# Softmax reciprocals moved from VectorE to GpSimd, as a power of minus one, in a fused attention and two-layer MoE kernel

## The chip, the cores and the metric

The kernel runs on one core of a Trainium2 chip. The core has five engines with queues of their own, each of which works in order: TensorE (PE, with its weight loads shown as PEld), VectorE (DVE), ScalarE (ACT), GpSimd (POOL) and SyncE (SP), which here issues most DMAs. The metric is the device time of one execution in microseconds; lower is better. Three runs of the kernel before gave 962.45, 959.7 and 960.58 us, a median of 960.58.

## The reference

Attention with a block mask, then two feed-forward layers. Cut to what matters:

```python
# q, k, v: 4 batches, 8 heads, 576 positions, 64 features
scores = q @ k^T / sqrt(64); masked where block_i < block_j (blocks of 64)
attn = exp(scores - max)
attn = attn / (sum(attn) + 1e-9)
x = attn @ v                                  # 2304 tokens x 512
g = softplus(x @ w_in);  x = g @ w_out        # 512 -> 2048 -> 512
xn = x / sqrt(mean(x^2) + 1e-6) * rms_g
out = (silu(xn @ w_gate) * (xn @ w_val)) @ w_out2   # 512 -> 1536 -> 512
```

The changed step is the division by the sum of the exponentials.

## The kernel before

The work is done in fp32 accuracy, by splitting operands into a high and a low part and adding three products. Attention is cut into 48 units (batch, group of 192 queries, pair of heads), each with 3 tiles of 128 rows (64 queries of two heads). The unit's scores are computed tile by tile (`s_tile`): matmuls into a PSUM bank, the negated row maximum on DVE (L831), exp on ACT with the row sum as a side output (L868), and then `s_norm`. The first 12 units are "whole": they run in plain fp32, their P tiles are transposed on TensorE (L919), and the row factor is applied at the end, by a small matmul that reads the factors `nm[:, 4:7]` of all three tiles in `pv_whole` (L951 to L957). `s_norm` runs once per whole unit, three columns wide, and once per tile in the other 36 units, one column wide: 12 + 108 = 120 times.

In the other units the factor scales P into fp16 parts right away (`s_split`): the high part on ACT (L892, 84 times) or DVE (L891, 24 times), and the low part on DVE (L895). A zero-fill of the odd half block goes to GpSimd (L889, L897). When the third tile is done, one DMA transposes the parts `pst` into `pt` (L905), and the products with V follow six tiles later (LAG_T = 6).

`s_norm` is two instructions: the sum plus 1e-9, times a constant, on GpSimd (L876), and the reciprocal on DVE (L877), in place in `nm`. Its readers take the cell `(nm, "r", i)`.

While attention for the next 384 tokens runs, the first feed-forward layer of the tokens before is on the same engines: `g1` and `g2` fill PE between the attention matmuls. Attention ends at about 340 us; then follow the rest of the first layer and the second.

Nothing is emitted in the order in which it is written. `Plan.op` records each operation with an engine, a cost in us, a key and the cells that it reads and writes. `Plan.emit` schedules the list on a model of the engines up to 12 times and emits the order with the shortest modelled end. In the model each GpSimd operation that is no DMA holds a port that it shares with the DVE operations marked `port=True`. Operations with alternatives (`op2`) get their engine there too. A changed cost or engine can therefore move any instruction of the program.

`tops` is a small constant tile; its columns 0 to 27 hold the gain vector and column maxima of weights.

Of the kernel before, what the change touches and what calls it, by code (L numbers as in the profile page):

```python
# [8 lines left out]
FP32 = mybir.dt.float32  # L9
# [6 lines left out]
ALU = mybir.AluOpType  # L16
# [68 lines left out]
class Plan:  # L85
# [12 lines left out]
    def op(self, eng, dur, key, fn, reads=(), writes=(), done=0.0, nbytes=0, after=(), alt=(), cols=0.0, port=False):  # L98
        i = len(self.ops)
        if port:  # L100
            self.shared.add(i)
        if eng == "PE":
            self.cols[i] = cols
        if self.pin:
            self.pins[i] = key - self.pin
        if alt:
            self.alts[i] = ((eng, dur, fn),) + tuple(alt)
        deps, starts = set(), set(after)
        for c in reads:
            deps.update(self.writers.get(c, ()))  # L110
        for c in writes:
            deps.update(self.readers.get(c, ()))
            deps.update(self.writers.get(c, ()))
        for c in list(reads) + list(writes):
            b = c[0] if isinstance(c, tuple) else c
            if isinstance(b, Buf):
                if b.first is None:
                    b.first = i
                    if isinstance(b.ring, Banks):
                        self.takes[i] = b  # L120
                    if b.older is not None:
                        self.reuse.append((i, b.older))
                    else:
                        deps.update(b.ring.before)
                    if b.prev is not None:
                        starts.add(b.prev.first)
                else:
                    starts.add(b.first)
                b.users.append(i)
        for c in writes:  # L130
            if self.readers.get(c):
                self.writers[c] = [i]
                self.readers[c] = []
            else:
                self.writers.setdefault(c, []).append(i)
        for c in reads:
            self.readers.setdefault(c, []).append(i)
        deps.discard(i)
        self.ops.append((eng, dur, key, fn, deps, starts - deps - {i}, done, nbytes))
        return i  # L140
# [191 lines left out]
def t_act(n, sbuf=True):  # L332
    return (0.092 if sbuf else 0.05) + n * 0.836e-3
# [38 lines left out]
def kernel(  # L372
# [12 lines left out]
    nc = tc.nc  # L385
# [22 lines left out]
    op = plan.op  # L408

    const = ctx.enter_context(tc.tile_pool(name="const", bufs=1))  # L410
# [26 lines left out]
        return get  # L437

    ones = const.tile([128, 128], FP32, name="ones")
    tops = const.tile([128, 28], FP32, name="tops")  # L440
    gvec = tops[:, 0:KD]
    x_dram = {j: dram.tile([128, KD, 2, BLK], FP32, name=f"xd{j}") for j in range(NB)}
    y_dram = {j: dram.tile([128, KD, BLK], FP32, name=f"yd{j}") for j in range(NB)}
# [33 lines left out]
    def load(key, dst, src, reads=(), writes=(), nbytes=0, after=(), dur=0.45):  # L477
        return op("SP", dur, key, lambda: nc.sync.dma_start(out=dst(), in_=src), reads, writes, done=1.0, nbytes=nbytes, after=after)  # L478
# [212 lines left out]
    def aop(*args, **kw):  # L691
        att_ops.append(op(*args, **kw))

    def whole(u):
        return u < 12
# [10 lines left out]
    def load_k0(p, key):  # L706
        for c0, c1, cell in ((0, 192, k_cell(p)), (192, S, k_rest)) if p == 0 else ((0, S, k_cell(p)),):
            part_ = lambda c0=c0, c1=c1: k0(p)[:, c0:c1]
            att_ops.append(load(key, part_, kT[0, p][:, c0:c1], writes=[cell], nbytes=512 * (c1 - c0)))
            aop("ACT", t_act(c1 - c0), key, lambda part_=part_: nc.scalar.mul(part_(), part_(), 0.125), [cell], [cell])  # L710
            key += 0.25
# [13 lines left out]
    def load_q(u, key):  # L725
        b, g, p = units[u]
        cell, t = q_slot(u)
        att_ops.append(load(key, t, qP[b, g, p], writes=[cell], nbytes=196608, dur=0.63))
# [59 lines left out]
    def small(kind, fn, key, reads, writes):  # L788
        e = {"DVE": ("DVE", 0.07, lambda: fn(nc.vector)), "POOL": ("POOL", 0.245, lambda: fn(nc.gpsimd))}
        aop2([e[k] for k in kind], key, reads, writes, False)  # L790
# [3 lines left out]
    def s_tile(u, ib, key, after):  # L794
# [51 lines left out]
        if not 0:  # L846
            for x in todo:
                if whole(u):
                    s_turn(u, x[0], x[1], x[4])
                    continue  # L850
                s_norm(u, x[0], x[0] + 1, x[4])
                s_split(u, x[0], x[1], x[4])
            if whole(u) and ib == NG - 1:
                s_norm(u, 0, NG, key)
        elif ib == NG - 1:
            s_norm(u, 0, NG, key)
            for x in done:
                s_split(u, x[0], x[1], x[4])
# [13 lines left out]
    def s_norm(u, i0, i1, key):  # L872
        nm, done = part[u]
        key += 0.3
        cells = [(nm, "s", i) for i in range(i0, i1)]
        small(("POOL",), lambda e: e.tensor_scalar(nm()[:, 4 + i0:4 + i1], nm()[:, 4 + i0:4 + i1], 1e-9, 1.0 if whole(u) else 2.0**-14, ALU.add, ALU.mult), key, cells, [(nm, "t", i0)])  # L876
        aop("DVE", 0.08, key, lambda: nc.vector.reciprocal(nm()[:, 4 + i0:4 + i1], nm()[:, 4 + i0:4 + i1]), [(nm, "t", i0)], [(nm, "r", i) for i in range(i0, i1)])  # L877

    def s_split(u, ib, n, key):
        b, g, p = units[u]  # L880
# [477 lines left out]
    def when(t):  # L1358
        return when_[t] if t < len(when_) else when_[-1] + (t - len(when_) + 1)

    load_k0(0, 0.0)
    load_q(0, 0.1)
    load_q(1, 0.2)
# [138 lines left out]
    for s in range(len(steps) + LAG):  # L1502
        key = t_2 + s * step2
        if s < len(steps):
            j, f, i0, i1 = steps[s]
# [17 lines left out]
        if s >= LAG:  # L1523
            j, f, i0, i1 = steps[s - LAG]
# [70 lines left out]
```

## Time and profile before

| | |
|---|---|
| median of 3 runs | 960.58 us (959.7 to 962.45) |
| the profiled execution's own time | 959.8 us |
| span of its trace | 958.0 us |
| PE busy | 945.1 us |
| DVE busy | 724.4 us |
| ACT busy | 599.2 us |
| POOL busy | 50.8 us |

The profile is of one execution. The span runs from its first to its last instruction, and 1.8 us of the execution's time lie around it. Busy time of PE is partly modelled, since matmuls are pipelined. A row of the profile names the line of the kernel, the engine, the operation and the tiles; L464 is the one line that issues every matmul.

### The profile page before, as it was taken

How to read it: one execution, taken by the hardware profiler on the slowest of the kernel's cores; microseconds unless marked ns; L12 is line 12 of the kernel's file. 1: busy time of each engine (PE TensorE's matmuls, PEld its weight loads, DVE VectorE, ACT ScalarE, POOL GpSimd, SP SyncE). 2: the span in 40 equal slices, each digit the busy share in tenths (PEclk: the TensorE clock that was granted, in tenths of full speed). 3: DMA queues.
4: the chain of work that ended last, by engine and by line, in shares of the span. 5: the costliest groups of instructions: out<-in, count | busy, mean ns of one | idle time of the engine just before them, and what ended most of it. 6: DMA issues, size and time to landing. Idle time of an engine off the chain costs nothing.

```text
span 958.0 us, 19816 instructions
## 1 busy us (share of the span) xinstructions
PE 945.1 (99%) x7652; PEld 841.4 (88%) x7652; DVE 724.4 (76%) x1667; ACT 599.2 (63%) x1348; POOL 50.8 (5%) x220
## 2 busy tenths in 40 slices
PE   7999999999999999999999999999999999999998
PEld 5799899999999999999999997788887788877885
DVE  6989999987999859989845577786877754455455
ACT  7998887776778858778723454656564643433332
POOL 1101211111121000000000000000000000000000
PEclk9999999999999999999999999999999999999999
DMA  8654768988878656977576022223321200235322
GB/s 291 204 173 149 188 176 186 247 213 233 205 190 205 173 182 220 340 273 241 192 273 220 1 92 90 80 91 100 114 78 34 78 34 2 78 109 195 127 67 89
DMA packets 127663, 149.28 MB, mean 156 GB/s; under 512 B 86096, under 2 KB 100176, under 8 KB 126032
## 3 DMA queue, kind: packets, MB, share of 16 engines
q1 hardware_dynamic: 126992, 141.72, 48.8%
q0 software_dynamic: 576, 6.29, 1.8%
q8 instruction: 60, 0.98, 0.4%
q14 instruction: 35, 0.29, 0.1%
HBM read 98.44 MB, written 29.10 MB: 133 GB/s over the span
## 4 chain that ended last, share of the span: by engine, by line
PE 73%; DVE 1%; DMA 0%; ACT 0%; issue 0%; DVEq 0%; SPq 0%
PE b L464 73%; DMA wraw<-in_w2gv_dram 0%; DVE t L1078 0%; DVE g L365 0%; DVE pst L895 0%; ACT P L868 0%; DVE nm L831 0%; DVE pst L891 0%; DVE khl L757 0%; DVE wraw L1318 0%; DVEq L1590 0%; SPq L478 0%; DVE nm L833 0%; DVE nm L877 0%; DVE tops L564 0%
## 5 line engine op out<-in xcount | busy, mean ns | idle before, releaser
L464 PE MATMUL b<-x,w 128*128 128x192 f16 (+1 forms) x4176 | 482.9, 272 | 1.0 <-ACT P L868 0.9
L464 PEld LDWEIGHTS <-w 128*128 128x128 f16 x3024 | 250.5, 98 | 7.5 <-issue 0.2
L464 PE MATMUL b<-g,w 128*128 128x384 f32 x1152 | 225.1, 337 | 0.0
L464 PEld LDWEIGHTS b<-x,w 128*128 128x128 f32 x1152 | 199.5, 188 | 4.5 <-ACT P L868 1.7
L464 PEld LDWEIGHTS b<-g,w 128*128 128x128 f32 x1152 | 200.0, 188 | 1.5
L464 PE MATMUL b<-w,g 128*128 128x512 f16 (+1 forms) x654 | 145.4, 377 | 0.0
L464 PEld LDWEIGHTS <-g 128*128 128x128 f16 x654 | 63.6, 98 | 68.1
L1237 DVE TENSOR_TENSOR m<-m 128x384 f32<-128x384 f32 x72 | 40.1, 557 | 89.7 <-ACT m L1249 88.8
L1249 ACT COPY m<-b 128x384 f32<-128x384 f32 x108 | 51.8, 479 | 79.7 <-PE b L464 78.9
L868 ACT ACTIVATE P<-b,nm 128x288 f32<-128x288 f32 (+8 forms) x160 | 79.8, 501 | 13.5 <-DVE nm L831 9.6
L831 DVE TENSOR_REDUCE nm<-b 128x1 f32<-128x288 f32 (+8 forms) x160 | 70.5, 450 | 15.0 <-PE b L464 14.6
L355 ACT CAST g<-t 128x384 fp32r<-128x384 f32 x96 | 49.0, 515 | 36.6 <-PE b L464 34.1
L365 DVE TENSOR_TENSOR g<-t,g 128x384 fp32r<-128x384 f32 x96 | 52.7, 553 | 22.3 <-ACT g L355 21.9
L464 PE MATMUL b<-khl,qbd 128*128 128x448 f32 (+7 forms) x360 | 68.3, 312 | 0.2 <-ACT P L868 0.2
L895 DVE SCALAR_TENSOR_TENSOR pst<-P,nm,pst 128x320 f16<-128x320 f32 (+8 forms) x108 | 58.4, 546 | 5.0 <-ACT pst L892 4.2
L464 PEld LDWEIGHTS b<-khl,qbd 128*128 128x128 f32 x360 | 56.5, 188 | 3.0 <-ACT P L868 1.4
L892 ACT ACTIVATE pst<-P,nm 128x384 f16<-128x384 f32 (+8 forms) x84 | 47.8, 579 | 8.3 <-DVE nm L877 5.1
L1258 ACT ACTIVATE t<-b,fac 128x384 f32<-128x384 f32 x36 | 20.9, 580 | 40.0 <-PE b L464 39.8
L1273 ACT CAST g<-t 128x384 f16<-128x384 f32 x36 | 18.4, 512 | 41.9 <-DVE t L1272 41.9
L876 POOL TENSOR_SCALAR nm<-nm 128x1 f32<-128x1 f32 (+1 forms) x120 | 31.7, 264 | 220.7 <-ACT P L868 167.9
L1072 ACT ACTIVATE t<-b 128x384 f32<-128x384 f32 x51 | 24.9, 488 | 28.6 <-PE b L464 28.5
L1235 DVE TENSOR_TENSOR m<-b,m 128x384 f32<-128x384 f32 x72 | 39.9, 554 | 0.0
(137 smaller groups left out, 1159.8 us busy)
## 6 DMA issues: line engine op xcount, KB each, us to landing
wraw<-in_w2gv_dram SPq DMA_DIRECT2D x41, 512.0 KB, 4.4
wraw<-in_w_dram SPq DMA_DIRECT2D x25, 512.0 KB, 4.3
wraw<-in_w2o_dram SPq DMA_DIRECT2D x16, 512.0 KB, 4.8
qf<-in_qP_dram SPq DMA_DIRECT2D x42, 192.0 KB, 2.8
y<-yd SPq DMA_DIRECT2D x10, 768.0 KB, 6.1
xd<-x SPq DMA_DIRECT2D x32, 192.0 KB, 3.4
x<-xd POOLq DMA_DIRECT2D x4, 1536.0 KB, 8.4
xnd<-x SPq DMA_DIRECT2D x4, 1344.0 KB, 8.6
```

The lines of the kernel that those rows point to most:

```text
L355: "ACT": ("ACT", t_act(n), lambda: nc.scalar.copy(dst(), src())),
L365: "DVE": ("DVE", t_dve(n), lambda: nc.vector.tensor_tensor(dst(), a(), b(), ALU.subtract)),
L464: nc.tensor.matmul(o, lhsT=l, rhs=r, start=start, stop=stop, **kw)
L831: aop("DVE", t_dve(cn), key, lambda sp=sp, col=col, cn=cn: nc.vector.tensor_reduce(nm()[:, col:col + 1], sp()[:, :cn], axis=AX.X, op=ALU.m ...
L868: aop("ACT", 0.24 + cn * 0.836e-3, key, lambda sp=sp, col=col, c0=c0, cn=cn: nc.scalar.activation(P()[:, c0:c0 + cn], sp()[:, :cn], ACTF.E ...
L876: small(("POOL",), lambda e: e.tensor_scalar(nm()[:, 4 + i0:4 + i1], nm()[:, 4 + i0:4 + i1], 1e-9, 1.0 if whole(u) else 2.0**-14, ALU.add, ...
L892: "ACT": ("ACT", t_act(n) + 0.09, lambda: nc.scalar.activation(hi(), pc(), ACTF.Copy, scale=r())),
L895: aop("DVE", t_dve(n, True), key, lambda: nc.vector.scalar_tensor_tensor(lo(), pc(), r(), hi(), ALU.mult, ALU.subtract), [P, (nm, "r", ib) ...
L1072: op("ACT", t_act(BLK, False) + (1.28 if not sp_op else 0.0), key - 5, lambda: nc.scalar.activation(e(), h()[:, :BLK], ACTF.Softplus), [h] ...
L1235: op("DVE", t_dve(BLK), k, lambda: nc.vector.tensor_tensor(dst(), a(), b(), alu), rd, wr, port=o_sb(rd))
L1237: op2([("DVE", t_dve(BLK), lambda: nc.vector.tensor_tensor(dst(), a(), b(), alu)), ("POOL", t_pool2(BLK), lambda: nc.gpsimd.tensor_tensor( ...
L1249: op("ACT", t_act(BLK, False), key + 1, lambda o=o, s=s: nc.scalar.copy(s(), ps(o)()), [o], [s])
```

## The change

The reciprocal on DVE is replaced by an elementwise power on GpSimd, with a column of -1.0 as exponent. The column lies in four new columns of `tops` and is filled once by a memset on GpSimd. The operation's cost for the planner goes from 0.08 on DVE to 0.3 on POOL; its cells stay, with "minus" as one more input.

```diff
-    tops = const.tile([128, 28], FP32, name="tops")
+    tops = const.tile([128, 32], FP32, name="tops")
...
         small(("POOL",), lambda e: e.tensor_scalar(nm()[:, 4 + i0:4 + i1], nm()[:, 4 + i0:4 + i1], 1e-9, 1.0 if whole(u) else 2.0**-14, ALU.add, ALU.mult), key, cells, [(nm, "t", i0)])
-        aop("DVE", 0.08, key, lambda: nc.vector.reciprocal(nm()[:, 4 + i0:4 + i1], nm()[:, 4 + i0:4 + i1]), [(nm, "t", i0)], [(nm, "r", i) for i in range(i0, i1)])
+        aop("POOL", 0.3, key, lambda: nc.gpsimd.tensor_tensor(nm()[:, 4 + i0:4 + i1], nm()[:, 4 + i0:4 + i1], tops[:, 28:28 + i1 - i0], ALU.pow), [(nm, "t", i0), "minus"], [(nm, "r", i) for i in range(i0, i1)])
...
+    op("POOL", 0.1, 0.0, lambda: nc.gpsimd.memset(tops[:, 28:32], -1.0), [], ["minus"])
     load_k0(0, 0.0)
```

## Rows read from the trace of the kernel before

**Rows 1.** The page's first part: engine, busy us, share of span, instructions.

```profile
PE 945.1 (99%) x7652; PEld 841.4 (88%) x7652; DVE 724.4 (76%) x1667; ACT 599.2 (63%) x1348; POOL 50.8 (5%) x220
```

**Rows 2.** Busy time by stretch: us, PE, PEld, DVE, ACT, POOL, clock, DMA.

```profile
0.00:20.00 20.00, 13.44 (x95) 9.67 (x95) 11.29 (x30) 14.96 (x44) 1.78 (x14) 1.00 0.91 319
...
250.00:300.00 50.00, 49.89 (x424) 47.87 (x423) 46.34 (x141) 40.83 (x116) 8.99 (x39) 1.00 0.86 214
...
60.00:340.00 280.00, 278.26 (x2233) 262.45 (x2232) 248.59 (x685) 225.11 (x595) 41.73 (x184) 1.00 0.77 198
```

**Rows 3.** The chain that ended last: start us, length us, what.

```profile
255.56 698.59 PE b L464 x5723
```

**Rows 4.** Waits from 20 to 340 us: waiter <- releaser: us, times, longest.

```profile
ACT P L868 <- DVE nm L831: 9.6, 16, 1.9
...
POOL pst L889 <- DMA pt<-pst: 19.7, 10, 5.3
...
ACT pst L892 <- DVE nm L877: 5.1, 11, 0.9
PEld b L464 <- ACT P L868: 4.2, 11, 1.2
...
DVE nm L877 <- POOL nm L876: 3.8, 10, 1.1
...
PE b L464 <- ACT P L868: 1.3, 3, 0.9
...
PEld L464 <- DMA pt<-pst: 1.1, 2, 0.7
...
PEld L464 <- DVE nm L877: 0.2, 1, 0.2
```

**Rows 5.** Groups by line: the reciprocal and the one-wide sum.

```profile
L877 DVE RECIPROCAL nm<-nm 128x1 f32<-128x1 f32 (+1 forms) x120 | 18.5, 156 | 4.9 <-POOL nm L876 4.4
...
L876 POOL TENSOR_SCALAR nm<-nm 128x1 f32<-128x1 f32 x108 | 27.2, 252 | 177.3 <-ACT P L868 146.2 <-DVE nm L870 28.6 <-DVE g L365 0.7
```

**Rows 6.** Timeline, sums and reciprocals: first pair, one between, last of 108.

```profile
85.64 0.63 POOL L876 TENSOR_SCALAR nm<-nm 128x1 f32<-128x1 f32 x1 [3.54 <-ACT P L868]
86.36 0.15 DVE L877 RECIPROCAL nm<-nm 128x1 f32<-128x1 f32 x1
...
155.10 0.19 POOL L876 TENSOR_SCALAR nm<-nm 128x1 f32<-128x1 f32 x1 [1.35 <-ACT P L868]
...
156.07 0.15 DVE L877 RECIPROCAL nm<-nm 128x1 f32<-128x1 f32 x1
156.14 0.44 DVE L831 TENSOR_REDUCE nm<-b 128x1 f32<-128x288 f32 x1
...
156.44 0.67 ACT L892 ACTIVATE pst<-P,nm 128x448 f16<-128x448 f32 x1
...
332.55 0.19 POOL L876 TENSOR_SCALAR nm<-nm 128x1 f32<-128x1 f32 x1 [2.43 <-DVE nm L870]
332.96 0.15 DVE L877 RECIPROCAL nm<-nm 128x1 f32<-128x1 f32 x1
```

**Rows 7.** Timeline, the sum beside a two-operand DVE instruction.

```profile
150.18 0.75 DVE L895 SCALAR_TENSOR_TENSOR pst<-P,nm,pst 128x512 f16<-128x512 f32 x1 [0.35 <-ACT pst L892]
...
159.41 0.75 DVE L895 SCALAR_TENSOR_TENSOR pst<-P,nm,pst 128x512 f16<-128x512 f32 x1
159.58 0.63 POOL L876 TENSOR_SCALAR nm<-nm 128x1 f32<-128x1 f32 x1 [3.17 <-DVE nm L870]
```

**Rows 8.** Timeline, the first unit.

```profile
8.26 0.19 POOL L876 TENSOR_SCALAR nm<-nm 128x3 f32<-128x3 f32 x1 [7.28 <-ACT P L868]
...
8.48 0.18 DVE L877 RECIPROCAL nm<-nm 128x3 f32<-128x3 f32 x1 [0.56 <-POOL nm L876]
...
11.66 0.52 PE L464 MATMUL b<-ones,nm 128*64 128x64 f32 x12
...
13.56 0.55 PE L919 MATMUL b<-ones,P 128*128 128x128 f32 x3 [1.38 <-ACT P L868]
```

## The prediction

> **What bounds the kernel now.** I read the busy times first. TensorE (PE) is busy in 945.1 us of the span, VectorE (DVE) in 724.4, ScalarE (ACT) in 599.2 and GpSimd (POOL) in 50.8 [rows 1]. Shares over the span mix stages, so next come the stretches [rows 2]. The changed lines run only while attention runs, up to 333 us. In the stretch from 60 to 340 us PE is busy for 278.26 of 280 us at a granted clock of 1.00, DVE for 248.59 and ACT for 225.11. From 250 to 300 us DVE is busy for 46.34 of 50. So PE sets the pace, and DVE is the next engine to run out of time. The reader is to see that PE's open idle time in that stretch is 280 - 278.26 = 1.74 us. The first 20 us hold 20 - 13.44 = 6.56 us more.
>
> The chain that ended last says the same from the other end [rows 3]. From 255.56 us on it is one piece of PE work, 698.59 us long. What a wait costs after 255.56 us did not decide the end in that execution. An edit in attention can only move the end by what it does to PE's waits before that, or by making a new one.
>
> Third, I asked who waited for whom from 20 to 340 us [rows 4]. PE's longest group of waits is for the exp on ACT, 1.3 us in 3 times. The weight loads (PEld) wait for the exp for 4.2 us and for the DMA transpose for 1.1 us. The exp itself waits for the row maximum on DVE (9.6 us in 16 times). So a freer DVE does have a way to PE: maximum earlier, exp earlier, PE's bank free earlier. The reciprocal stands as a releaser of weight loads with 0.2 us, once. ACT's scaling of P (L892) waits for it for 5.1 us in 11 times out of 84, and only 10 times in 120 did DVE sit idle for the sum of GpSimd, 3.8 us in all.
>
> **The change part by part.** *Reciprocals taken off DVE.* 120 of them go, 18.5 us of recorded busy time, 156 ns each [rows 5]. But DVE starts its next instruction before one has ended: in the example of [rows 6] the reciprocal starts at 156.07 and the maximum behind it at 156.14. So each one costs the DVE queue 0.07 us. That is 120 x 0.07 = 8.4 us, of which the 108 one-wide ones of the later units make 7.6 us. This lies on an engine that is not the bound. It is worth to PE at most what PE waits for the chain through DVE and exp.
>
> *Powers added to GpSimd.* 120 instructions with two operands in SBUF. The trace has no power and no two-operand instruction on GpSimd. From below: the sum's own small instruction on GpSimd has a mean of 252 ns one-wide [rows 5], and 0.19 us when nothing disturbs it [rows 6]; a power can hardly be cheaper. From above, the long cases of the one-wide sum take 0.63 us, at 85.64 and 159.58 [rows 6, 7], and a power with such a delay and twice the sum's own work on top would come to 0.63 + 2 x 0.19, about 1 us. The diff's own cost line says 0.3, a number for ordering and no measurement. I take 0.35 us, nearer the undisturbed row, since only one value in each partition is worked on, and keep 0.19 and 1.0 for the range. The load on GpSimd, 120 x 0.35 = 42 us, fits: from 60 to 340 us it is busy for 41.73 of 280 us [rows 2].
>
> *The latency from sum to factor.* Now the reciprocal stands in the queue of a busy DVE. I took the gap from the end of each sum to the start of its reciprocal for all 108 one-wide pairs; first and last are in [rows 6] (gaps 0.09 and 0.22), and so is one with 0.78. The mean is 0.45 us. With its own 0.155 the factor is there 0.61 us after the sum. Afterwards the power starts right behind the sum on the same engine, say 0.05 us later, the gap that an undisturbed hand-over in this trace shows ([rows 8], 8.45 to 8.48, gives 0.03). That makes 0.05 + 0.35 = 0.40 us: 0.2 us sooner. With 0.19 it is 0.24, with 1.0 it is 1.05, which is 0.44 us later. The break-even is a power of 0.56 us.
>
> *The port.* At 159.58 the sum takes 0.63 us, and ends as the two-operand DVE instruction beside it (L895 from 159.41, 0.75 us) ends. The L895 with the same shape at 150.18, which has no GpSimd work beside it, takes 0.75 us as well [rows 7]. So here GpSimd waits and DVE does not pay. The Trainium skill's "GPSIMD Engine Reference", section "Specifications", says that GpSimd shares its SBUF interfaces with VectorE and contends with instructions that have two SBUF inputs; this trace agrees on the 0.63 against 0.19, and the rule speaks against the change: it would put a second instruction of each tile into that contention. By the rows a power that meets one is delayed by up to 0.44 us, and by none where the sum has just waited it out, as it comes directly behind it. I count 0.06 us per power, the mean excess of the sum (252 - 192), inside the 0.35. For DVE I count nothing.
>
> *Order in the queues.* The planner is given another engine, 0.3 in place of 0.08, and a dependence between two GpSimd instructions. It lists the whole program anew, so any engine's order may shift, and with it the choice between DVE and ACT for the scaling. I can't cost that from rows. I allow 3 us either way, a little over what all PE idle time of the stretch amounts to. The memset of the -1 column falls into GpSimd's idle first 8 us [rows 8] and costs nothing; without that cover it would cost one instruction of 0.2 us.
>
> *First units.* The factor of the first unit is ready at 8.66 and first read by PE at 11.66 [rows 8]: 3.0 us of cover over the longest price taken above. No loss there.
>
> *Sum.* The freed DVE time and the shorter hand-over make the exp come a little sooner. I give PE back the 1.3 us that it waited for the exp [rows 4], and none of the weight loads' 4.2, because those loads overlap running matmuls. From the profiled execution's own 959.8 us this gives 958.5. The three runs have a median of 960.58, 0.8 above it; on that scale it is 960.6 - 1.3 = 959.3 us. A measurement of this kernel tells about 0.3%, 2.9 us, from no change; so this is no change.
>
> **The rivals.** *DVE is the hidden bound* (faster). For it: 46.34 of 50 us in the densest stretch, and exp waiting for DVE 9.6 us. If all of PE's 1.3 and the weight loads' 4.2 us behind the exp go, the time is 960.6 - 5.5 = 955.1. Against it: the stretch shows only 1.74 us of open PE idle time, and from 255.56 us nothing but PE decides.
>
> *The power is slow* (slower). Price 1.0 us, decisive from 0.56 up. The factor then comes 0.44 us later than now, and behind ACT's L892 stand, in order, the next exps and the copies that feed PE. 84 x 0.44 = 37 us of ACT waits at worst, against 280 - 225.11 = 54.9 us of ACT idle time [rows 2]. ACT would have little left; if one in seven of these microseconds reaches PE, an estimate, that is 5.3 us: 965.9. Against it: most scalings start later than the factor is ready, as only 11 of 84 waited for it.
>
> *Head of line on GpSimd* (slower). The zero-fills of pst wait in the same queue for the DMA transpose, 19.7 us in 10 times, longest 5.3 [rows 4]. If the new order puts such a fill between a sum and its power, the power waits with it. A few waits of 5.3 us, each covered in part by the lag of six tiles between scores and values, would give about 4 us: 964.6. Before, the reciprocal on DVE could not be caught so, only the sum.
>
> *First use pays once* (no change still). The first power may take longer than the rest, if its code has to be fetched. Unit 0 has 3.0 us of cover between 8.66 and 11.66; what goes beyond it delays PE, less what PE would have idled anyway (1.38 us at 13.56 [rows 8]). It leaves the band of 2.9 us only where the first power takes over 3.0 + 2.9 = 5.9 us with nothing absorbed; a first power between 3.0 and 5.9 us gives up to 963.5. Against it: the first sum on GpSimd took 0.19 us [rows 8], with no pause in front of it that the trace puts down to code. The Trainium skill's "GPSIMD Engine Reference", section "Instruction dispatch", gives the first call of a freshly loaded GpSimd kernel about 6 us that a profile shows no instruction for; by it the time would be an estimated 963.5 before anything is absorbed, and no run here shows it yet.
>
> **How the numbers follow.** Forecast (within 0.3%): 0.43, with the first-use rival's 0.05 in the same band: same 0.48. DVE as hidden bound, or an order that falls out well: faster 0.29. Slow power 0.13 and head of line or a worse order 0.10: slower 0.23. The range goes from just under the DVE case, 954.5, to the slow-power case, 965.9, rounded to 966. The likeliest case alone is 957.7 to 962.
>
> **What would show it.** Right: the powers last 0.25 to 0.45 us; ACT's wait for the factor (L892) falls under 5.1 us; DVE from 60 to 340 us has 7 to 16 us less recorded busy time (0.07 us each if overlaps are counted once, 0.155 if not); PE idle there stays between 0.5 and 3 us; the sum's own duration stays near 0.25. Wrong: powers of 0.6 us or more, and ACT's waits for GpSimd above 15 us in the list of waits; fills ahead of powers in the timeline; PE waiting for the transposes; or an attention stage that ends more than 3 us from 340 us in either direction.

## The result and the profile after

The changed kernel takes 967.66 us (median of 6 runs, 964.5 to 969.7) against 960.9 us: a ratio of 1.0063, interval 1.0048 to 1.0078. It is slower by about 6 us. The forecast was 959.3 us and no change; 967.66 lies above the range's 966.

The page's first part, of the kernel after:

```profile
PE 949.6 (98%) x7652; PEld 842.3 (87%) x7652; DVE 716.3 (74%) x1544; ACT 600.0 (62%) x1351; POOL 125.8 (13%) x341
```

DVE did lose its load: 716.3 us against 724.4 [rows 1], 8.1 us less, where 8.4 were forecast. GpSimd went from 50.8 to 125.8 us, 75 us more, where 42 were forecast. Busy time by stretch (us, PE, PEld, DVE, ACT, POOL, clock, DMA share, GB/s) answers to [rows 2]:

```profile
0.00:20.00 20.00, 13.73 (x87) 9.36 (x88) 10.28 (x23) 14.30 (x43) 4.67 (x18) 0.91 0.90 323
60.00:340.00 280.00, 277.07 (x2192) 259.82 (x2191) 242.03 (x572) 228.48 (x601) 108.60 (x295) 1.00 0.76 195
```

From 60 to 340 us PE is idle for 2.93 us against 1.74, and issues 41 matmul records fewer. GpSimd is busy for 108.60 of 280 us. Its groups by line are next; L877 is the power, one and three columns wide, L876 the sum. They answer to [rows 5]:

```profile
L877 POOL TENSOR_TENSOR nm<-nm,tops 128x1 f32<-128x1 f32 x108 | 64.6, 601 | 7.5
L876 POOL TENSOR_SCALAR nm<-nm 128x1 f32<-128x1 f32 x108 | 27.8, 257 | 121.7 <-ACT P L868 94.0 <-DVE nm L870 18.1 <-DVE am L770 4.3
L877 POOL TENSOR_TENSOR nm<-nm,tops 128x3 f32<-128x3 f32 x12 | 11.6, 964 | 0.7
```

A power has a mean of 601 ns where 350 were taken. Over the 108 pairs, the way from the end of the sum to the end of the power is 0.80 us on average; to the end of the reciprocal it was 0.60 us. The waits from 20 to 340 us (us in total, times, longest) answer to [rows 4]:

```profile
ACT pst L892 <- POOL nm L877: 16.3, 27, 1.4
...
POOL pst L889 <- DMA pt<-pst: 12.9, 8, 3.3
...
ACT P L868 <- DVE nm L831: 10.7, 17, 1.4
...
PEld b L464 <- ACT P L868: 5.8, 11, 1.4
...
DVE pst L891 <- POOL nm L877: 4.2, 10, 1.0
...
PE b L464 <- ACT P L868: 2.6, 4, 1.1
```

The reader is to see the wait of ACT's scaling for the factor, 5.1 us before and 16.3 now, and below it PE's own wait for the exp doubled, 1.3 to 2.6. Of these 2.6 us, though, 2.0 fall before 105 us, where it was 0.2 before the change and where few of the powers lie. The exp's wait for the maximum has not shrunk (9.6 to 10.7), although DVE is freer.

That is not the whole of it, though. L1017 copies a unit's result from PSUM, so its first and last start date the first split unit and the last. The source view of before and after (durations, then first and last start in us):

```profile
L1017 ACT ACTIVATE x<-b,dall x36: 397/416/457, 105.0 to 343.2; 128x192 fp32r<-128x192 f32 x36
```

```profile
L1017 ACT ACTIVATE x<-b,dall x36: 397/418/462, 108.6 to 349.7; 128x192 fp32r<-128x192 f32 x36
```

The changed kernel is 3.6 us late by the first of these copies, when 22 of the 120 powers have run, and 6.5 us late at the last. Something else besides the power is slow, and the new listing of the program is the suspect.

### The profile page after: what moved, and what is told of

Its sections match the earlier page's. It is cut to its first block, busy times and chain, and to the rows that moved or that the text cites. A ratio compares the mean times of both kernels' runs of the same rounds, so it can differ in the third digit from the quotient of the medians.

```text
span 966.0 us, 19810 instructions
## 1 busy us (share of the span) xinstructions
PE 949.6 (98%) x7652; PEld 842.3 (87%) x7652; DVE 716.3 (74%) x1544; ACT 600.0 (62%) x1351; POOL 125.8 (13%) x341
## 4 chain that ended last, share of the span: by engine, by line
PE 54%; DVE 5%; ACT 3%; DMA 2%; issue 1%; POOL 0%; DVEq 0%; ACTq 0%
PE b L464 54%; DVE w L607 1%; DMA m<-in_w2o_dram 1%; DVE wg L365 1%; DMA wraw<-in_w_dram 1%; DVE w L365 1%; DMA m<-in_w2gv_dram 1%; DVE g L365 1%; ACT wraw L505 1%; DVE wg L508 0%; ACT wa L506 0%; ACT w L355 0%; DVE wa L508 0%; ACT w L606 0%; ACT g L355 0%
## 5 line engine op out<-in xcount | busy, mean ns | idle before, releaser
L464 PE MATMUL b<-g,w 128*128 128x384 f32 x1152 | 228.2, 339 | 1.2 <-DVE y L1132 0.9
L868 ACT ACTIVATE P<-b,nm 128x288 f32<-128x288 f32 (+8 forms) x160 | 79.6, 501 | 13.2 <-DVE nm L831 10.7
L877 POOL TENSOR_TENSOR nm<-nm,tops 128x1 f32<-128x1 f32 (+1 forms) x120 | 76.2, 637 | 8.2
L895 DVE SCALAR_TENSOR_TENSOR pst<-P,nm,pst 128x64 f16<-128x64 f32 (+8 forms) x108 | 57.7, 547 | 12.0 <-ACT pst L892 11.5
L892 ACT ACTIVATE pst<-P,nm 128x128 f16<-128x128 f32 (+8 forms) x89 | 51.1, 580 | 17.3 <-POOL nm L877 16.3
L876 POOL TENSOR_SCALAR nm<-nm 128x1 f32<-128x1 f32 (+1 forms) x120 | 31.6, 263 | 155.2 <-ACT P L868 116.3
L505 ACT ACTIVATE wraw<-wraw 128x512 int32<-128x512 uint32 x50 | 33.9, 679 | 11.7 <-DMA wraw<-in_w_dram 7.1
```

What stands on the lines that cost most here:

```text
L464: nc.tensor.matmul(o, lhsT=l, rhs=r, start=start, stop=stop, **kw)
L505: op("ACT", t_act(CW), prio, lambda: nc.scalar.activation(lw().bitcast(I32), lw(), ACTF.Copy, scale=0.874 * 2.0**-29, bias=0.5), [raw], [( ...
L868: aop("ACT", 0.24 + cn * 0.836e-3, key, lambda sp=sp, col=col, c0=c0, cn=cn: nc.scalar.activation(P()[:, c0:c0 + cn], sp()[:, :cn], ACTF.E ...
L877: aop("POOL", 0.3, key, lambda: nc.gpsimd.tensor_tensor(nm()[:, 4 + i0:4 + i1], nm()[:, 4 + i0:4 + i1], tops[:, 28:28 + i1 - i0], ALU.pow) ...
L892: "ACT": ("ACT", t_act(n) + 0.09, lambda: nc.scalar.activation(hi(), pc(), ACTF.Copy, scale=r())),
L895: aop("DVE", t_dve(n, True), key, lambda: nc.vector.scalar_tensor_tensor(lo(), pc(), r(), hi(), ALU.mult, ALU.subtract), [P, (nm, "r", ib) ...
```

## The experiments

Two theories stood from here. *Price*: the power takes GpSimd too long, the factor is late, ACT and with it PE wait. *Order*: the planner, told another engine and cost, lists a program that is worse whoever computes the reciprocal. "Old order" below means that the planner was told the kernel before, so that PE, ACT, SP and the rest of DVE keep that kernel's order; only the instruction behind the reciprocal's entry is another. "New order" is the listing of the changed kernel. Ratios are to runs of the kernel before on the same chip, each with its 95% interval.

**Old order, with the power.**

```diff
-aop("DVE", 0.08, key, lambda: nc.vector.reciprocal(...), ...)
+aop("DVE", 0.08, key, lambda: nc.gpsimd.tensor_tensor(..., tops[:, 28:28 + i1 - i0], ALU.pow), ...)
...
+nc.gpsimd.memset(tops[:, 28:32], -1.0)     # ahead of everything
```

> The planner is told the old story (0.08 us on DVE), so TensorE, ScalarE, SyncE and the rest of DVE keep the order of the kernel before; only the reciprocal itself runs as a power on GpSimd. Theory price (the power lasts 0.54 to 0.64 us where 0.3 was planned, ACT and DVE wait for it, TensorE idles): 965 to 969 us, and the 16 us of waits of L892 for the power come back. Theory order (the newly listed order is worse whoever computes the reciprocal): 959 to 962 us.

Measured: 967.72 us, 1.007 (1.0055 to 1.0085). The price theory's number. The loss starts where the one-wide powers start, as the copies show:

```profile
L1017 ACT ACTIVATE x<-b,dall x36: 400/415/453, 105.7 to 351.7; 128x192 fp32r<-128x192 f32 x36
```

At the first copy it is 0.7 us late, at the last 8.5. How it comes about is best seen in one stretch, first in the kernel before (timeline: start us, length, engine, line):

```profile
109.22 0.15 DVE L877 RECIPROCAL nm<-nm 128x1 f32<-128x1 f32 x1
...
109.87 0.19 ACT L868 ACTIVATION_READ_ACCUMULATOR P<-b,nm 128x1 f32 x1
109.96 0.95 ACT L892 ACTIVATE pst<-P,nm 128x256 f16<-128x256 f32 x2
...
110.15 0.19 POOL L876 TENSOR_SCALAR nm<-nm 128x1 f32<-128x1 f32 x1 [0.63 <-ACT P L868]
...
111.41 0.16 DVE L877 RECIPROCAL nm<-nm 128x1 f32<-128x1 f32 x1
...
111.68 0.61 ACT L892 ACTIVATE pst<-P,nm 128x384 f16<-128x384 f32 x1
111.83 1.49 PE L464 MATMUL b<-x,w 128*128 128x384 f32 x7 [0.93 <-ACT P L868]
```

Then the same tiles in the old order with the power:

```profile
109.95 1.44 POOL L877 TENSOR_TENSOR nm<-nm,tops 128x1 f32<-128x1 f32 x2
...
110.59 0.19 ACT L868 ACTIVATION_READ_ACCUMULATOR P<-b,nm 128x1 f32 x1
...
110.91 1.07 ACT L892 ACTIVATE pst<-P,nm 128x256 f16<-128x256 f32 x2
111.34 0.31 POOL L897 MEMSET pst<- 128x256 f16 x1
...
111.73 0.26 POOL L876 TENSOR_SCALAR nm<-nm 128x1 f32<-128x1 f32 x1
...
112.04 0.20 POOL L889 MEMSET pst<- 128x128 f16 x1
...
112.21 0.76 POOL L877 TENSOR_TENSOR nm<-nm,tops 128x1 f32<-128x1 f32 x1
...
112.90 0.44 PE L464 MATMUL b<-x,w 128*128 128x384 f32 x1 [1.28 <-ACT P L868]
113.00 0.62 ACT L892 ACTIVATE pst<-P,nm 128x384 f16<-128x384 f32 x1 [0.16 <-POOL nm L877]
```

Before, the row sum is read out by 110.06, and GpSimd takes it up 0.09 us later. With the power, the row sum is there at 110.78, but GpSimd is in the second of two powers and then in a fill; the tile's sum starts at 111.73, 0.95 us later, another fill follows, and the power ends at 112.97. From row sum to factor it is 2.2 us, where it was 1.5. ACT's scaling of this tile waits for it and starts at 113.00. PE's wait for the exp there is 1.28 us in place of 0.93, but it ends at 112.90, before this power does. It goes back to the two powers ahead, from 109.95 to 111.39: ACT's scalings of their tiles start 0.32 us after the start of the row sum's read-out, where it was 0.09, and take 1.07 us in place of 0.95, and only then comes the next exp. So in this stretch the tiles come in a burst, and GpSimd's queue is the thing that is late.

**New order, reciprocal back on DVE; new order, a cheap instruction on GpSimd.**

```diff
 # in the changed kernel; the entry stays ("POOL", 0.3), only what it issues changes
-lambda: nc.gpsimd.tensor_tensor(..., ALU.pow)
+lambda: nc.vector.reciprocal(...)                                       # one kernel
+lambda: nc.gpsimd.tensor_scalar(..., constant, 1.0, ALU.mult, ALU.mult)  # the other
```

> The order of the changed kernel on every engine, but the reciprocal runs on DVE as before (0.155 us), at the place in the list that the power had. Theory price: 959 to 962 us, as the slow instruction is gone. Theory order: 966 to 969 us, with the split of the first tile (L895) still starting near 95 us and not near 89.

> The order of the changed kernel, the instruction stays on GpSimd, but is a multiplication by a constant (about 0.2 us) in place of the power: the reciprocal is left out of the computation, factors and results are others. Theory price: 959 to 962 us. Theory order: 966 to 969 us. Between the two only the duration on GpSimd differs from the changed kernel.

Measured: with the reciprocal on DVE 967.09 us, 1.0069 (1.0052 to 1.0085); with the cheap instruction 963.63 us, 1.0028 (1.0017 to 1.0039). Neither theory alone gives both: the first lies in the range of the order theory, the second between the two ranges. The cheap one leaves 2.7 us of loss with no power in the kernel: that is the new order. The first is worse than that by about 4 us, although nothing slow is left on GpSimd and the old order carries the same reciprocals. The new order was listed without them on DVE; that this is the reason is not shown, as ACT waits for the factor there for only 7.0 us, near the 5.1 of the kernel before.

Where the order loses can be seen by stretch (as in [rows 2]). From 20 to 105 us, the kernel before, the changed kernel, and the cheap instruction in the new order:

```profile
20.00:105.00 85.00, 84.26 (x675) 72.80 (x673) 78.97 (x201) 78.92 (x208) 10.71 (x42) 1.00 0.55 170
20.00:105.00 85.00, 81.26 (x634) 68.83 (x632) 76.62 (x175) 75.32 (x194) 20.80 (x53) 1.00 0.53 164
20.00:105.00 85.00, 81.47 (x632) 69.01 (x631) 77.21 (x177) 75.88 (x198) 13.17 (x56) 1.00 0.55 168
```

PE is idle for 0.74, 3.74 and 3.53 us there, while only 19 and 20 of their 120 powers or multiplications run by then. Over all kernels of this document, those below included, it is 0.6 to 1.0 us in the old order and 1.6 to 4.1 in the five other listings, whatever computes the factor. From 105 to 350 us it is the other way round. The kernel before, the changed kernel, the cheap instruction in the new order, and the power in the old order:

```profile
105.00:350.00 245.00, 243.29 (x1949) 230.98 (x1946) 210.22 (x585) 191.05 (x504) 36.01 (x161) 1.00 0.80 200
105.00:350.00 245.00, 243.65 (x1958) 230.39 (x1957) 203.68 (x480) 192.29 (x514) 97.98 (x266) 1.00 0.79 197
105.00:350.00 245.00, 244.72 (x1967) 232.10 (x1966) 202.95 (x482) 192.64 (x512) 59.68 (x264) 1.00 0.79 199
105.00:350.00 245.00, 239.49 (x1881) 224.24 (x1878) 202.64 (x476) 186.50 (x497) 95.86 (x261) 0.99 0.79 196
```

Here PE is idle for 1.71, 1.35, 0.28 and 5.51 us. In the old order the power's price shows as 3.8 us of idle time of PE, in the new order as 1.1 us (1.35 against 0.28).

**Changed kernel, the planner told the measured durations.**

```diff
-aop("POOL", 0.3, key, ...
+aop("POOL", 0.55 if i1 - i0 == 1 else 0.95, key, ...
```

> The changed kernel with the measured durations told to the planner (0.55 us one column wide, 0.95 three wide, in place of 0.3), so the order is listed anew around the real price. Theory price: part of the loss goes, 961 to 965 us. Theory order: a new order is a new draw, anywhere from 957 to 970 us, and no reason to lie near the kernel before.

Measured: 967.13 us, 1.0068 (1.0053 to 1.0083). A listing that knows the price does not avoid it. The expectation of the price theory, that a part of the loss would go, was wrong.

**Old order, a cheap instruction on GpSimd.** As the first experiment, with the multiplication by a constant in place of the power.

> The order of the kernel before, and on GpSimd behind the sum a multiplication by a constant (about 0.2 us) in place of the power; the reciprocal is left out of the computation. Beside the old order with the power (967.7 us) only the duration on GpSimd differs. Theory price: the loss goes, 958.5 to 962 us, L892 waits 3 to 6 us for it. Theory hand-over (it is the move to GpSimd that costs, whatever its duration: one more instruction in its queue, its port): 965 to 968 us.

Measured: 961.05 us, 1.000 (0.9987 to 1.0014). Moving the step to GpSimd is harmless when it is short, and the 8 us taken off DVE buy nothing either.

**Two new listings of the kernel before.**

```diff
-aop("DVE", 0.08, key, lambda: nc.vector.reciprocal(...
+aop("DVE", 0.07, key, lambda: nc.vector.reciprocal(...     # and 0.10 in a second kernel
```

> Nothing but the planner's cost of the reciprocal changes, from 0.08 to 0.07 us: the same instructions on the same engines, listed anew. Theory order (a new listing alone moves the time by some us): up to 5 us from 960.9 in either direction, most likely upwards. If a new listing is harmless: 959.5 to 962.5 us.

> As the one before with a cost of 0.10 us: a second redraw of the order with no other change. Theory order: up to 5 us from 960.9 in either direction, and not the same as the first. If a new listing is harmless: 959.5 to 962.5 us.

Measured: 964.6 us, 1.0042 (1.0025 to 1.0058), and 964.2 us, 1.0029 (1.0015 to 1.0042). The same instructions, but for the choice between ACT and DVE for the scaling of P (84 on ACT before, 80 and 79 in these two), and 3 to 4 us slower for a hundredth or two in a cost, as the order theory expected.

**Doses of GpSimd time, all in the old order.** Two and three multiplications one behind the other in place of the power; and the power alone, straight on the row sum, without the sum's instruction:

```diff
-lambda: nc.vector.reciprocal(...)
+lambda: [nc.gpsimd.tensor_scalar(..., constant, 1.0, ALU.mult, ALU.mult), ...]   # two, three
...
-e.tensor_scalar(..., 1e-9, 2.0**-14, ALU.add, ALU.mult)                         # the power alone:
+None                                                                            # no sum
```

> The order of the kernel before; in place of the power two multiplications by constants stand one behind the other on GpSimd, about 0.43 us together (the reciprocal is left out of the computation). The forecast's break-even of 0.56 us: no loss, 959.5 to 962 us. Theory urgent hand-over (what counts is not the mean way of 0.61 us but the 0.2 us in which DVE delivered when ACT was already waiting): loss in proportion to the duration above 0.2, 962.5 to 965.5 us, and waits of L892 between 6 and 15 us.

> As the one before with three multiplications, about 0.65 us, as long as the power. If only the duration counts: 966 to 969 us and waits of L892 near 15 us, as with the power in the old order. If the power does something else beside lasting (its two operands in SBUF, its port): under 965 us.

> The order of the kernel before; the power runs on GpSimd straight on the row sum and the sum's own instruction is left out (without the 1e-9 and with the factor 2^-14 moved to the scale of V). The way from row sum to factor loses about 0.2 us against the old order with the power, and GpSimd 30 us of load. Theory urgent hand-over: part of the loss comes back, 962 to 965.5 us. If the way from row sum to factor does not matter, or GpSimd's duration alone does: 967 us as with the sum.

Measured: two, 966.41 us, 1.0052 (1.0034 to 1.0069); three, 981.52 us, 1.0217 (1.0198 to 1.0236); the power alone, 960.51 us, 0.9997 (0.9984 to 1.0011). None of the three lies in a range that was expected of it: two lie above both, three far above, as the multiplications lasted 0.75 us a tile and not 0.65, and the power alone lies below both. Groups by line give what one tile takes of GpSimd, sum and factor together. One multiplication, the power alone, two multiplications, the sum with the power, three multiplications:

```profile
L876 POOL TENSOR_SCALAR nm<-nm 128x1 f32<-128x1 f32 x108 | 27.8, 258 | 150.5 <-ACT P L868 123.0 <-DVE nm L870 24.6 <-DVE am L770 0.8
L877 POOL TENSOR_SCALAR nm<-nm 128x1 f32<-128x1 f32 x108 | 25.8, 243 | 7.2
```

```profile
L877 POOL TENSOR_TENSOR nm<-nm,tops 128x1 f32<-128x1 f32 x108 | 65.0, 605 | 145.1 <-ACT P L868 119.0 <-DVE nm L870 22.4 <-issue 2.9
```

```profile
L877 POOL TENSOR_SCALAR nm<-nm 128x1 f32<-128x1 f32 x216 | 53.3, 249 | 16.1
L876 POOL TENSOR_SCALAR nm<-nm 128x1 f32<-128x1 f32 x108 | 27.3, 253 | 120.1 <-ACT P L868 97.6 <-DVE nm L870 19.7 <-DVE am L770 0.4
```

```profile
L877 POOL TENSOR_TENSOR nm<-nm,tops 128x1 f32<-128x1 f32 x108 | 65.5, 610 | 7.3
L876 POOL TENSOR_SCALAR nm<-nm 128x1 f32<-128x1 f32 x108 | 27.4, 254 | 121.0 <-ACT P L868 97.6 <-DVE nm L870 20.5 <-DVE am L770 0.4
```

```profile
L877 POOL TENSOR_SCALAR nm<-nm 128x1 f32<-128x1 f32 x324 | 80.6, 250 | 25.0
L876 POOL TENSOR_SCALAR nm<-nm 128x1 f32<-128x1 f32 x108 | 26.7, 247 | 107.7 <-ACT P L868 85.3 <-DVE nm L870 19.4
```

| GpSimd's part of a one-wide tile, old order | busy us per tile (sum over both groups / 108) | ratio to before |
|---|---|---|
| sum alone (kernel before) | 0.25 | 1 |
| sum and one multiplication | 0.50 | 1.000 |
| power alone | 0.60 | 0.9997 |
| sum and two multiplications | 0.75 | 1.0052 |
| sum and power | 0.86 | 1.007 |
| sum and three multiplications | 0.99 | 1.0217 |

It costs nothing up to 0.60 us a tile, and between 0.60 and 0.75 it begins to cost. The table counts busy time alone; with the idle time before each further instruction (the last number of the L877 rows) GpSimd is held for 0.56, 0.60, 0.90, 0.93 and 1.22 us from the second row to the last. The power is nothing special: two multiplications hold GpSimd about as long and cost 5.0 us against its 6.8, and the power without the sum in front of it is free.

The time from the end of the row sum to the factor sorts the same kernels as well. Its mean over the 102 one-wide tiles whose row sum can be told from the waits is 0.97 us before, 0.82 with one multiplication and 0.72 with the power alone, all free, and 1.25, 1.26 and 1.67 us with two, with sum and power, and with three. ACT's wait for the factor goes along, shown here for the power alone, for two multiplications, for the sum with the power, and for three multiplications (waits from 20 to 345 us):

```profile
ACT pst L892 <- POOL nm L877: 4.0, 6, 1.0
...
PE b L464 <- ACT P L868: 1.1, 2, 0.9
```

```profile
ACT pst L892 <- POOL nm L877: 14.9, 28, 1.2
```

```profile
ACT pst L892 <- POOL nm L877: 15.4, 24, 1.3
```

```profile
ACT pst L892 <- POOL nm L877: 32.5, 47, 1.5
...
PE b L464 <- ACT P L868: 8.7, 13, 1.5
```

**Old order, the power in the first 12 units only.**

```diff
-lambda: nc.vector.reciprocal(...)
+lambda: nc.gpsimd.tensor_tensor(..., ALU.pow) if whole(u) else nc.vector.reciprocal(...)
```

> The order of the kernel before; only the 12 three-wide reciprocals of the first units run as a power on GpSimd (about 0.95 us each), the 108 one-wide ones stay on DVE. The first units read their factors 2 to 3 us later by the trace of before: 960 to 962 us by either theory. If the three-wide powers or a first call were part of the price: 963 us or more, with a drift that begins before 100 us.

Measured: 961.51 us, 1.0005 (0.9993 to 1.0018). The three-wide powers, about 0.95 us each, cost nothing.

**Old order, no sum on GpSimd, reciprocal on DVE.**

```diff
-e.tensor_scalar(..., 1e-9, 2.0**-14, ALU.add, ALU.mult)
+None
```

> The order of the kernel before; the reciprocal stays on DVE and the sum's instruction on GpSimd is left out, so that DVE takes the reciprocal of the row sum directly. Left out are the addition of 1e-9 and the factor 2^-14, which moves to the scale of V. Theory price, turned around (a shorter way from the row sum to the factor gives time back): 956 to 960 us and L892 waiting under 4 us. If that way is not what TensorE waits for in the old order: 959.5 to 962 us.

Measured: 960.78 us, 0.9995 (0.9982 to 1.0007). With the whole hop through GpSimd gone, nothing is won. The way from row sum to factor became little shorter by it, 0.92 us against 0.97, because the reciprocal still stands in DVE's queue; the power alone makes it 0.72 and wins nothing either, so the old order has no use for a shorter way to the factor.

**The power alone, in the new order, and in an order of its own.**

```diff
 # changed kernel, the sum issues nothing;   second kernel: the sum's entry is removed as well and
 # the planner is told 0.55 and 0.95 us
```

> The order of the changed kernel with the power straight on the row sum; the sum's own instruction is left out (without the 1e-9, the factor 2^-14 moved to the scale of V). In the old order this took the whole price away (960.5 us). If price and order are two separate losses: the order's stays, as with the cheap multiplication in the new order, 962 to 965 us. If the new order loses only because of the slow way to the factor: 960 to 962 us.

> The power straight on the row sum, listed anew with its measured durations (0.55 and 0.95 us) and without the sum's instruction: one try at a version that beats both kernels. DVE has 8 us less to do and the way to the factor is as long as before. If a fitting listing could use that: 956 to 959.5 us. If a new listing costs 3 to 4 us as the two redraws did: 962 to 966 us.

Measured: 964.02 us, 1.0024 (1.0009 to 1.004), and 963.77 us, 1.0027 (1.0016 to 1.0039). With the price gone, the order's loss stays, 2.3 us; and one more listing, made for the power alone, is no better than the others.

## Why the prediction was wrong

*What bounds the kernel.* Right: PE sets the pace. In the old order with the power, what is lost can be seen as PE's waits for the exp behind ACT's scaling: its idle time from 105 to 350 us rises from 1.71 to 5.51 us. In the changed kernel only 1.1 us of idle time show the power, against the cheap instruction in the same order. 3.0 us more than before lie between 20 and 105 us, and 4.5 us more (949.6 against 945.1) stand as busy time of PE, which is partly modelled and of which 1.7 us go with a lower clock at the start (last section). By which way the rest of the power's share reaches the end there stays open.

*DVE's relief.* Right in size (8.4 forecast, 724.4 - 716.3 = 8.1 us of busy time), wrong in worth. From 60 to 340 us it is 6.6 us (248.59 to 242.03), just under the 7 to 16 named as a sign of being right. Of the 1.3 us given back to PE, none was seen: the cheap instruction in the old order takes as much off DVE and stands at 1.000. The exp's wait for the maximum did not fall.

*The power.* 0.35 us was taken, 0.60 measured (0.95 three wide). The mis-sized term is the first step that failed, but not the one that decides: by the prediction's own break-even of 0.56 us a power of 0.60 would have cost next to nothing. The upper bound of 1.0 did hold it.

*The break-even.* This is the step that failed and decided. For the hand-over from sum to factor it set an undisturbed 0.05 us plus the power's own duration against a mean of 0.61 us, and it called GpSimd's load fitting, as 42 us had room in 280. So it put nothing in the sum for waiting in GpSimd's own queue, and had the factor 0.2 us sooner. The measured way from sum to factor after the change is 0.80 us, 0.2 later: 0.60 for the power, 0.08 for the undisturbed hand-over, and the rest because before 27 of the 108 one-wide powers a fill or a neighbouring tile's sum or power stands in between. With 0.80 in place of 0.40 the prediction's own comparison of means would have said later. The added duration was put at the factor's door alone, whereas it also delays the next tile's sum, as the stretch at 111.73 shows. In the old order all this costs 6.8 us. Whether each single microsecond is lost by the queue being held or by the longer hand-over when ACT already waits, the runs don't tell apart: both grow along the same axis. Two of the prediction's own signs of being wrong came, powers of 0.6 us and ACT's waits above 15 us.

*The rivals.* The slow power came, with its place (behind L892, 5.1 to 16.3 us) and its side, at a smaller price than it had been given and with more loss. It let one in seven microseconds of ACT's waits reach PE; in the old order ACT's scaling waits 9.8, 10.3 and 27.4 us longer with two multiplications, the power and three, and the kernels are 5.0, 6.8 and about 20 us slower, more than half of it. Its condition, decisive from 0.56 us, was met by the measured 0.60 us; its chance of 0.13 was too low because the hand-over seemed to say that 0.60 is harmless. Head of line came in another form than forecast: not by longer waits of fills for the DMA transpose (19.7 us before, 12.9 now), but by fills, sums and powers that are themselves in the way. The first use costs nothing: here is unit 0 of the changed kernel, to be held against [rows 8]:

```profile
8.21 0.19 POOL L876 TENSOR_SCALAR nm<-nm 128x3 f32<-128x3 f32 x1 [7.20 <-ACT P L868]
8.56 0.88 POOL L877 TENSOR_TENSOR nm<-nm,tops 128x3 f32<-128x3 f32 x1
...
11.40 0.52 PE L464 MATMUL b<-ones,nm 128*64 128x64 f32 x12
```

The first power lasts 0.88 us, where the three-wide ones have a mean of 0.96, and PE reads its factor at 11.40, no later than the 11.66 of before. The 6 us that the Trainium skill's "GPSIMD Engine Reference", section "Instruction dispatch", gives to the first call of freshly loaded code are not seen in this trace; the kernel with the power in the first units only, at 1.0005, agrees.

*The port.* Right: DVE did not pay. L895 lasts 547 ns on average in the changed kernel and 546 before.

*The order.* "3 us either way" had the right size, but only the slower side came, and in the sum it stood at nothing. PE's idle time of 1.74 us, to which the prediction tied it, bounds what an order can win and not what it can lose. This term too failed: the new order costs 2.3 to 2.7 us, before 105 us. Five kernels without the slow way, in four new listings, came out 2.3 to 4 us slower and none faster: the two redraws, the power alone in its own order, and the cheap instruction and the power alone in the new order. That the order before is an uncommonly good one is argued from this, not shown.

*The sum of both.* The loss of about 6 us is made of a new order, 2.3 to 2.7 us by the two kernels that keep the new order and drop the price, and of the power's price, the rest, some 3.5 us. Measured against the third kernel of that order, with the reciprocal on DVE (6.6 us slower), the power would cost nothing; so the split holds for a short instruction on GpSimd in the power's place. The parts don't add up over orders: in the old order, which was listed for an instruction of 0.08 us, the same power costs 6.8 us. Why the new order bears it better, and why it bears the reciprocals on DVE worse, stays open.

## What to carry to other kernels

An engine that is idle for most of a stretch is not free for a chain of small dependent instructions: count what one unit of work holds of its queue, and add to its duration the waits behind its neighbours, which the mean load does not show. Where one list is scheduled as a whole, measure a redraw with no other change beside the change itself, and the change in the old order; without both, 2 to 4 us of order are taken for the edit's. Folding two steps into one (here the power without the sum) took the slow instruction's price away as fully as a short instruction in its place did; neither made the kernel faster than before.

## What was not expected of the hardware

A power on GpSimd takes 0.60 us for one value in each partition and 0.96 for three, so most of it does not depend on the size. Dependent instructions on GpSimd follow each other at about 0.07 us (7.3 us of idle time before 108 powers).

TensorE's granted clock can fall after a gap at the start. In the changed kernel PE idled 2.18 us before 14.10 (before the change 1.38 us before 13.56 [rows 8], with a clock of 1.00 [rows 2]), and the stretches behind it show the lower level, 1.2 GHz, in part or whole (busy time by stretch, the clock is the third number from the end):

```profile
12.00:14.00 2.00, 0.00 (x0) 0.00 (x0) 2.00 (x5) 1.99 (x6) 0.00 (x0) 1.00 1.04 408
14.00:16.00 2.00, 1.90 (x7) 1.39 (x8) 2.00 (x7) 2.00 (x7) 1.47 (x3) 0.64 1.03 397
16.00:18.00 2.00, 2.00 (x5) 0.85 (x4) 1.93 (x4) 2.00 (x11) 0.64 (x3) 0.51 1.08 406
18.00:20.00 2.00, 2.00 (x30) 1.68 (x29) 1.55 (x3) 2.00 (x8) 0.80 (x2) 1.00 0.99 388
```

That is 0.36 x 2 + 0.49 x 2 = 1.7 us at full speed, part of the 3.6 us by which this execution is late at its first split unit. It is no explanation of the result: another run of the changed kernel had a mean clock of 1.000 and took 968.45 us.
